# FFN2 for pairs of token tiles by seven products in a fused attention and FFN kernel

## The chip, the cores and the metric

The kernel runs on one core of a Trainium2 chip. The core has TensorE (PE: matmuls, and weight loads beside them as PEld), VectorE (DVE), ScalarE (ACT), GpSimd (POOL) and SyncE (SP, here a queue that issues DMAs). Each engine works through its own list of instructions in order and waits on semaphores for the others. The metric is the device time in microseconds (us), the median of several runs.

## The reference, cut to what matters

There are 8 batches, 12 heads, 448 positions and a head width of 64; the FFN takes the 3584 tokens of all batches, 768 wide, to 2048 and back.

```python
scores = q @ k.T / sqrt(64)
attn   = max(scores, 0) ** 2 / 448
x      = (attn @ v) with heads put side by side     # 3584 x 768
h      = x @ w_in                                   # 3584 x 2048
g      = max(h, 0) + alpha * min(h, 0)
out    = g @ w_out                                  # 3584 x 768
```

## The kernel before, in words

**Stages.** A "quad" is four heads of one batch; there are three in a batch (NG) and 24 in all. For a quad the kernel loads q, k and v as bf16 (`load_qk`, `load_v`: DMAs of GpSimd's queue), turns q and k so that the head width lies on partitions, computes seven score chunks of 128 x 896 (`score_mm`, L184), passes each through a relu on ScalarE (L193) or VectorE (L195), squares it on VectorE (L203), multiplies by v (`attnv`, L213), and writes xT with the scale, half on ScalarE (L223), half on VectorE (L224).

For a batch, `f1` then runs 16 times (index ff, one block of 128 of d_ff each): six matmuls of 448 columns (L247), `neg` = relu(-h) on ScalarE (L255), and gT = beta * neg + h on VectorE (L256). Two batches share one gT, of 128 x 16 x 896 in bf16, which holds seven token tiles of 128. `f2` takes one token tile and one of two column ranges (256 or 512 wide, `COLS`), accumulates 16 matmuls into a bank (L272), copies it with ScalarE to an `o` tile (L274) and stores it in two halves through Sync's queue (L280).

**Turning q and k.** Quads 0 to 4 are transposed on TensorE. From quad 5 on `turn_dma` first copies q and k into a `perm` tile with VectorE (L170, two copies), and then Sync issues one transposing DMA from `perm` into T (L172). `perm` has three buffers. Three one-element GpSimd copies to `landed` (L425, L473, L488) hold GpSimd's queue until the transposes of quads 5, 6 and 8 have landed; the next loads stand behind them.

**Order of the work.** The order is written out by hand (`manual_schedule`), and every engine runs its instructions in the order of the code. From batch 2 on, FFN1 of a batch is cut by two runs of three score chunks (before ff 6 and ff 12) and has two `prepare` calls (ff 1 and 9), each of which turns one quad and loads another. The FFN2 stage after it has three bursts, one for each quad of the next batch: three score chunks with relus on ScalarE, VectorE, ScalarE ("ADA"), the product with v, two more chunks ("AD"), and then the squares of the five chunks. The stage after an even batch works on token tiles 0 to 2 and the one after an odd batch on tiles 3 to 6. Batch 7 has no bursts.

**PSUM.** There are eight banks of 512 F32. `take_bank` and `take_pair` choose the bank, or the even-aligned pair, that was taken least recently; a score chunk and an attention product each need a pair, FFN1 and FFN2 a bank. `hold` sets a bank aside.

## Time and profile before

| What | Value |
|---|---|
| Median of 3 runs | 386.65 us (385.65 to 386.66) |
| Profiled execution, first to last instruction | 384.0 us |
| Granted TensorE clock | 1.000 |
| TensorE busy | 374.1 us |
| VectorE, ScalarE, GpSimd busy | 266.2, 207.6, 68.9 us |
| FFN2 stage after batch 2 (137.52 to 160.62) | 23.10 us, VectorE busy 17.71 |
| FFN2 stage after batch 3 (180.38 to 208.68) | 28.30 us, VectorE busy 17.79 |
| FFN2 stage after batch 6 (319.35 to 341.31) | 21.96 us, VectorE busy 11.03 |
| FFN2 of batch 7 (from 359.47) | about 21.1 us |

The profile shows one execution. Its own time is known as the span from the first instruction to the last; the medians are of other executions and include what lies around the span. In a line of a group the fields are line, engine, operation, output and inputs, shape and count, then the busy time in us, the mean ns of one, and the engine's idle time just before them with what ended it. In a line of the timeline they are start, duration, line, operation and count, with the idle time before in square brackets. Matmuls overlap, so that the mean of one is longer than the distance between two starts.

### The profile page before, as it was taken

The page shows a single profiled execution, that of the slowest core. Times are in us where ns is not written, and L with a number is a line of the kernel's source. Part 1 is how long each engine was busy: PE and PEld are TensorE (multiplying, and loading weights), DVE is VectorE, ACT ScalarE, POOL GpSimd, SP SyncE. Part 2 cuts the span into 40 slices and gives each one's busy share as a digit, 9 for nine tenths or more (in the row PEclk, how much of TensorE's full clock was granted, in tenths as well). Part 3 has the DMA queues.
Part 4 walks back from the last instruction along what each step waited for, and adds up shares of the span by engine and source line. Part 5 has one row for each costly group of instructions (what it writes and reads, how often), then busy time and mean ns, then how long its engine had stood idle before and what let it go on. Part 6 is the DMA issues. An engine that isn't in the chain of part 4 may idle for free.

```text
span 384.0 us, 7838 instructions
## 1 busy us (share of the span) xinstructions
PE 374.1 (97%) x3171; PEld 205.3 (53%) x3192; DVE 266.2 (69%) x423; ACT 207.6 (54%) x335; POOL 68.9 (18%) x105
## 2 busy tenths in 40 slices
PE   6799999999999999999999999999999999999996
PEld 5454565555544455545565455544556445645554
DVE  3987988777657988688656887779855788526300
ACT  4988687445643754455444656546544475434321
POOL 8566050506402202022200222020000000000000
PEclk9999999999999999999999999999999999999999
DMA  9999989999995667488292772946035300120023
GB/s 145 192 204 202 186 127 199 171 178 203 224 172 109 108 113 114 105 134 119 48 167 60 134 120 53 165 76 120 15 86 88 77 1 15 43 68 2 14 68 85
DMA packets 73556, 43.29 MB, mean 113 GB/s; under 512 B 40368, under 2 KB 70064, under 8 KB 73520
## 3 DMA queue, kind: packets, MB, share of 16 engines
q0 software_dynamic: 27136, 22.58, 39.8%
q1 hardware_dynamic: 45952, 19.88, 26.8%
q8 instruction: 25, 0.41, 0.5%
q10 hardware_dynamic: 432, 0.33, 0.3%
q14 instruction: 11, 0.09, 0.1%
HBM read 45.62 MB, written 11.01 MB: 147 GB/s over the span
## 4 chain that ended last, share of the span: by engine, by line
PE 95%; DVE 2%; issue 1%; POOL 0%; ACT 0%; ACTq 0%; POOLq 0%; DVEq 0%
PE psum L247 38%; PE psum L272 38%; PE psum L184 9%; PE psum L213 8%; DVE at L203 1%; PE psum L146 1%; DVE T L165 1%; PE psum L162 1%; DVE rl L195 0%; POOL kraw L131 0%; ACT osb L274 0%; ACTq L280 0%; POOL ident masks.py:199 0%; POOL ident masks.py:197 0%; POOLq masks.py:199 0%
## 5 line engine op out<-in xcount | busy, mean ns | idle before, releaser
L272 PE MATMUL psum<-w_out,gT 128*128 128x256 bf16 (+3 forms) x891 | 149.8, 322 | 1.1
L247 PE MATMUL psum<-xT,w_in_sb 128*128 128x448 bf16 x768 | 149.8, 353 | 0.0
L272 PEld LDWEIGHTS <-gT 128*128 128x128 bf16 x912 | 86.8, 98 | 64.2 <-issue 8.2
L247 PEld LDWEIGHTS <-w_in_sb 128*128 128x128 bf16 x768 | 73.7, 98 | 72.8 <-issue 5.3
L256 DVE SCALAR_TENSOR_TENSOR gT<-neg,beta_sb,psum 128x448 bf16<-128x448 f32 x128 | 83.4, 676 | 33.8 <-ACT neg L255 33.6
L255 ACT ACTIVATE neg<-psum 128x448 f32<-128x448 f32 x128 | 69.2, 546 | 60.3 <-PE psum L247 59.2
L193 ACT ACTIVATE rl<-psum 128x896 bf16<-128x896 f32 x112 | 97.7, 930 | 1.4 <-PE psum L184 1.4
L203 DVE TENSOR_TENSOR at<-rl 128x896 bf16<-128x896 bf16 x162 | 90.5, 616 | 0.0
L195 DVE TENSOR_SCALAR rl<-psum 128x896 bf16<-128x896 f32 x56 | 60.8, 1085 | 40.4 <-PE psum L184 40.3
L274 ACT COPY osb<-psum 128x256 f32<-128x256 f32 (+3 forms) x57 | 26.9, 473 | 104.7 <-PE psum L272 97.6
L184 PE MATMUL psum<-T 64*64 64x448 bf16 x672 | 45.4, 356 | 2.1 <-DVE T L165 1.1
L100 POOL DMA_DIRECT2D qraw<-in_q_dram x23 | 16.6, 722 | 136.2 <-DVE perm L170 131.7
L213 PE MATMUL psum<-at,vraw 64*64 64x448 bf16 x672 | 36.2, 350 | 0.0
L184 PEld LDWEIGHTS <-T 64*64 64x64 bf16 x672 | 16.8, 105 | 21.0 <-issue 13.6
L213 PEld LDWEIGHTS <-vraw 64*64 64x64 bf16 x672 | 21.0, 106 | 11.7 <-issue 1.5
L224 DVE TENSOR_SCALAR xT<-psum 128x448 bf16<-128x448 f32 x24 | 15.0, 624 | 14.8 <-PE psum L213 11.0
L107 POOL DMA_DIRECT2D vraw<-in_v_dram x24 | 17.5, 732 | 4.6 <-PE psum L184 1.4
L100 POOL DMA_DIRECT2D kraw<-in_k_dram x23 | 16.7, 726 | 1.9 <-issue 1.4
L223 ACT ACTIVATE xT<-psum 128x448 bf16<-128x448 f32 x24 | 13.4, 560 | 2.3 <-PE psum L213 2.3
L170 DVE COPY perm<-qraw 128x896 bf16<-128x896 bf16 x19 | 11.6, 610 | 0.0
L170 DVE COPY perm<-kraw 128x896 bf16<-128x896 bf16 x19 | 11.6, 608 | 0.0
L117 POOL DMA_DIRECT2D w_in_sb<-in_moe_w_in_dram x16 | 10.0, 634 | 5.5 <-DMA w_in_sb<-in_moe_w_in_dram 2.3
(24 smaller groups left out, 41.6 us busy)
## 6 DMA issues: line engine op xcount, KB each, us to landing
out_dram<-osb SPq DMA_DIRECT2D x54, 128.0 KB, 2.4
vraw<-in_v_dram POOLq DMA_DIRECT2D x24, 224.0 KB, 8.5
qraw<-in_q_dram POOLq DMA_DIRECT2D x23, 224.0 KB, 4.7
kraw<-in_k_dram POOLq DMA_DIRECT2D x23, 224.0 KB, 6.9
out_dram<-osb SPq DMA_DIRECT2D x56, 64.0 KB, 2.3
w_in_sb<-in_moe_w_in_dram POOLq DMA_DIRECT2D x16, 192.0 KB, 8.1
w_out<-in_moe_w_out_dram POOLq DMA_DIRECT2D x4, 512.0 KB, 10.3
w_out<-in_moe_w_out_dram POOLq DMA_DIRECT2D x4, 256.0 KB, 8.6
```

What stands on the lines that cost most here:

```text
L100: nc.gpsimd.dma_start(out=t.rearrange("p m j d -> p m (j d)"), in_=flat[:, 2 * g:2 * g + 2])
L170: nc.vector.tensor_copy(p[:, i], raw.pop((n, name)).rearrange("p s j d -> p j s d"))
L184: nc.tensor.matmul(ps[64 * c:64 * c + 64, r, :S], t[64 * r:64 * r + 64, 1, j, 64 * c:64 * c + 64], t[64 * r:64 * r + 64, 0, :, 64 * c:64 * ...
L193: nc.scalar.activation(rl, ps[:, :, :S], ACTF.Relu)
L195: nc.vector.tensor_scalar(rl, ps[:, :, :S], 0.0, None, ALU.max)
L203: nc.vector.tensor_tensor(a, rl, rl, ALU.mult)
L213: nc.tensor.matmul(ps[64 * s:64 * s + 64, r, :S], vv[64 * r:64 * r + 64, s, j, :], a[64 * r:64 * r + 64, s], start=(j == 0), stop=(j == NJ ...
L247: nc.tensor.matmul(ps, w_in_sb[:, km // 2, km % 2, bass.ts(ff, 128)], xT[b][:, km // 2, km % 2, :], start=(km == 0), stop=(km == KM - 1))
L255: nc.scalar.activation(neg, ps, ACTF.Relu, scale=-1.0)
L256: nc.vector.scalar_tensor_tensor(gT[b // 2][:, ff, (b % 2) * S:(b % 2) * S + S], neg, beta_sb[:, ff:ff + 1], ps, ALU.mult, ALU.add)
L272: nc.tensor.matmul(ps, gT[sb][:, ff, bass.ts(c, 128)], w_out_sb[h][:, ff, lo:hi], start=(ff == 0), stop=(ff == KF - 1))
L274: nc.scalar.copy(o[:, lo:hi], ps)
```

## The change

FFN2 of batches 2 to 7 goes through a new class `Pair` for pairs of token tiles. With a pair's gT split in four quarters (two tiles a and b, two halves of d_ff) and w_out split in four (two halves of d_ff, two halves of the 768 columns), a product of two by two blocks is made with seven block products and not eight (the Winograd form of Strassen's scheme). Each block product is eight matmuls of 384 columns. Four sums and differences of gT quarters are made on VectorE for each pair (`mix`), four of w_out once (`weight_mix`, in eight pieces, in the stage after batch 1). The results are gathered by accumulating products in three PSUM banks (x, y, z) and by adding the copy m1 or the sums u2 and u3 with VectorE (`plus`, five for each pair); ScalarE copies twice for each pair. There are three pairs for each two batches; the seventh token tile still goes through `f2`. x and y are one bank pair, held from p1 to p4; z is an ordinary `take_bank`.

Of the relus from batch 2 on only the third of each first burst stays on VectorE ("AAD", "AAA", then "AA", "AAA"); FFN1 has two runs, of three and two chunks (two and two in batch 2). The copies into `perm` go to GpSimd for quads 9 and later. `w_out_sb` is one tile. Several pools get fewer buffers; `perm` has one, not three. Two new pools come in, u (4) and S (4); S also takes some of the early `at` tiles, and the first q tiles come from the o pool.

```diff
-    perm_pool = ctx.enter_context(tc.tile_pool(name="perm", bufs=3))
+    perm_pool = ctx.enter_context(tc.tile_pool(name="perm", bufs=1))
-    rl_pool = ctx.enter_context(tc.tile_pool(name="rl", bufs=7))
-    at_pool = ctx.enter_context(tc.tile_pool(name="at", bufs=12))
+    rl_pool = ctx.enter_context(tc.tile_pool(name="rl", bufs=6))
+    at_pool = ctx.enter_context(tc.tile_pool(name="at", bufs=10))
-    neg_pool = ctx.enter_context(tc.tile_pool(name="neg", bufs=3))
-    o_pool = ctx.enter_context(tc.tile_pool(name="o", bufs=10))
+    neg_pool = ctx.enter_context(tc.tile_pool(name="neg", bufs=2))
+    o_pool = ctx.enter_context(tc.tile_pool(name="o", bufs=6))
+    u_pool = ctx.enter_context(tc.tile_pool(name="u", bufs=4))
+    S_pool = ctx.enter_context(tc.tile_pool(name="S", bufs=4))
...
+    def hold_pair():
+        lo = min((0, 2, 4, 6), key=lambda i: (max(taken[i], taken[i + 1]), i))
+        taken[lo] = taken[lo + 1] = 10**9
+        return lo
...
-            nc.vector.tensor_copy(p[:, i], raw.pop((n, name)).rearrange("p s j d -> p j s d"))
+            (nc.gpsimd if n > 2 * NG + 2 else nc.vector).tensor_copy(p[:, i], raw.pop((n, name)).rearrange("p s j d -> p j s d"))
...
+        def mix(self, *which):
+            for i in which:
+                t = self.s[i] = S_pool.tile([128, KH, 128], BF16, tag="S", name="S")
+                x, y, op = {1: (self.a21, self.a22, ALU.add),
+                            2: (self.s.get(1), self.a11, ALU.subtract),
+                            3: (self.a11, self.a21, ALU.subtract),
+                            4: (self.a12, self.s.get(2), ALU.subtract)}[i]
+                nc.vector.tensor_tensor(t, x, y, op)
+        def mm(self, ps, left, right, start):
+            for i in range(KH):
+                nc.tensor.matmul(ps, left[:, i], right[:, i], start=(start and i == 0), stop=(i == KH - 1),
+                                 skip_group_check=not start)
+        def p1(self):
+            self.xy = hold_pair()
+            self.x, self.y = psum[:, self.xy, :NH], psum[:, self.xy + 1, :NH]
+            self.mm(self.x, self.a11, w_out_sb[:, :KH, :NH], True)
+            self.m1 = self.kept()
+            nc.scalar.copy(self.m1, self.x)
+        def p6(self):
+            self.mm(self.y, self.s[2], w_mix[1], True)
+            self.u2 = self.plus(self.y, self.m1, self.kept())
+        def p7(self):
+            self.mm(self.y, self.s[3], w_mix[2], False)
+            self.u3 = self.plus(self.y, self.m1, self.kept())
+        def p5(self):
+            self.z = take_bank()[:, :NH]
+            self.mm(self.z, self.s[1], w_mix[0], True)
+        def c22(self):
+            store(self.sb, self.tb, NH, d_model, self.plus(self.z, self.u3))
+        def p2(self):
+            self.mm(self.x, self.a12, w_out_sb[:, KH:, :NH], False)
...
+        def p4(self):
+            self.mm(self.y, self.a22, w_mix[3], False)
+            take(self.xy, 2)
+            store(self.sb, self.tb, 0, NH, self.plus(self.y, self.m1))
+        def p3(self):
+            self.mm(self.z, self.s[4], w_out_sb[:, KH:, NH:], False)
+            store(self.sb, self.ta, NH, d_model, self.plus(self.z, self.u2))
+        def tail(self):
+            self.p7(); self.p5(); self.c22(); self.p2(); self.p4(); self.p3()
...
         if b % 2 == 0:
+            p = Pair(sb, 0, 1)
+            p.mix(1, 2)
+            if b + 2 < B:
+                f2(sb, 2, 0)
+            p.mix(3, 4)
+            burst(n0, "AAD", "AAA")
+            prepare(n0 + 4)
+            p.p1()
+            p.p6()
+            burst(n0 + 1, "AA", "AAA")
+            if b + 2 < B:
+                p.tail()
+                burst(n0 + 2, "AA", "AAA")
+                f2(sb, 2, 1)
...
+        elif not last:
+            p, r = Pair(sb, 3, 4), Pair(sb, 5, 6)
+            p.mix(1, 2, 3, 4)
+            burst(n0, "AAD", "AAA")
+            prepare(n0 + 4)
+            p.p1()
+            p.p6()
+            burst(n0 + 1, "AA", "AAA")
+            p.tail()
+            r.mix(1, 2, 3, 4)
+            r.p1()
+            r.p6()
+            burst(n0 + 2, "AA", "AAA")
+            r.tail()
         else:
+            p, r = Pair(sb, 2, 3), Pair(sb, 4, 5)
+            p.mix(1, 2, 3, 4)
+            p.p1(); p.p6(); p.p5(); p.p2(); p.p7(); p.c22()
+            f2(sb, 6, 0)
+            p.p4(); p.p3()
+            r.mix(1, 2, 3, 4)
+            r.p1(); r.p6(); r.p5(); r.p2(); r.p7(); r.c22(); r.p4(); r.p3()
+            f2(sb, 6, 1, parts=((0, 384), (384, 512)))
```

In the diff some calls that stand on lines of their own are put on one line.

## The prediction, made before the result was known

> **What bounds the kernel now.** I read the page's busy shares and its chain first, then the groups by shape, then the timeline of one FFN2 stage on all engines, then the Vector and Sync queues around the four transposing transfers of the first stages. The page:
>
> ```profile
> span 384.0 us, 7838 instructions
> ...
> PE 374.1 (97%) x3171; PEld 205.3 (53%) x3192; DVE 266.2 (69%) x423; ACT 207.6 (54%) x335; POOL 68.9 (18%) x105
> ...
> PE 95%; DVE 2%; issue 1%; POOL 0%; ACT 0%; ACTq 0%; POOLq 0%; DVEq 0%
> ```
>
> TensorE is busy 97% and carries 95% of the chain: a matmul saved is time saved, and a TensorE wait is time lost, since nothing gives it back. The groups by shape (busy us, mean ns):
>
> ```profile
> L272 PE MATMUL psum<-w_out,gT 128*128 128x512 bf16 x411 | 95.8, 379 | 1.1
> L203 DVE TENSOR_TENSOR at<-rl 128x896 bf16<-128x896 bf16 x162 | 90.5, 616 | 0.0
> ...
> L256 DVE SCALAR_TENSOR_TENSOR gT<-neg,beta_sb,psum 128x448 bf16<-128x448 f32 x128 | 83.4, 676 | 33.8 <-ACT neg L255 33.6
> ```
>
> A mean includes the pipeline; what counts is the spacing of starts. The timeline of the stage after FFN1 of batch 3 (start, us):
>
> ```profile
> 180.38 1.91 PE L272 MATMUL psum<-w_out,gT 128*128 128x256 bf16 x16
> 180.58 0.55 ACT L255 ACTIVATE neg<-psum 128x448 f32<-128x448 f32 x1 [0.59 <-PE psum L247]
> 181.16 0.68 DVE L256 SCALAR_TENSOR_TENSOR gT<-neg,beta_sb,psum 128x448 bf16<-128x448 f32 x1 [0.28 <-ACT neg L255]
> ...
> 182.22 0.76 PE L184 MATMUL psum<-T 64*64 64x448 bf16 x12
> ...
> 182.65 1.73 ACT L193 ACTIVATE rl<-psum 128x896 bf16<-128x896 f32 x2
> ...
> 182.81 1.50 PE L213 MATMUL psum<-at,vraw 64*64 64x448 bf16 x28
> 182.84 1.09 DVE L195 TENSOR_SCALAR rl<-psum 128x896 bf16<-128x896 f32 x1 [1.00 <-PE psum L184]
> ...
> 184.13 0.55 PE L184 MATMUL psum<-T 64*64 64x448 bf16 x8
> ```
>
> The last gT of FFN1 is ready 1.46 us after TensorE has left FFN1 (180.38 to 181.84); a score chunk costs TensorE 0.20, the attention product 1.33 (182.81 to 184.13); a relu starts 0.43 after its chunk, and two on ScalarE take 1.73. No engine is late here. Vector, Sync and GpSimd in batch 1:
>
> ```profile
> 63.71 0.61 DVE L170 COPY perm<-qraw 128x896 bf16<-128x896 bf16 x1
> ...
> 71.44 0.61 DVE L170 COPY perm<-qraw 128x896 bf16<-128x896 bf16 x1
> ```
> ```profile
> 64.91 2.46 SPq L172 DMA_TRANSPOSE T<-perm  x1
> ```
> ```profile
> 67.40 0.18 POOL L473 COPY landed<-T 1x1 bf16<-1x1 bf16 x1 [12.41 <-DMA T<-perm]
> 67.85 2.23 POOL L122 DMA_DIRECT2D w_out<-in_moe_w_out_dram  x3 [0.27 <-issue]
> ...
> 87.35 0.18 POOL L488 COPY landed<-T 1x1 bf16<-1x1 bf16 x1 [14.42 <-DMA T<-perm]
> ```
>
> Quad 6's transpose has landed at 67.4; quad 7's copy was made at 63.7, into another of three buffers.
>
> **TensorE saves 11.9.** A 256-wide pass of 16 matmuls takes 1.84 (180.38 to 182.22), a 512-wide one 3.46 (337.85 to 341.31): 5.30 a tile, 10.60 a pair. A 384-wide pass lies midway, 2.65, so a product of 8 costs 1.325, and 7 cost 9.27. Nine pairs (three for each two batches): 9 x 1.33 = -11.9. Attention and FFN1 issue the same matmuls.
>
> **Stage starts cost 10.2.** Everything below is counted from TensorE's end of FFN1. Vector must end gT (1.46), then the four operand additions, before the one relu that stays on it ("D" third in the first burst). An addition is a square (spacing 0.535) on 1024 in place of 896 elements: 0.61; the second waits for the first's result, so they run 1.5 to 4.0 and the relu to 5.1. ScalarE's relus are done earlier. The burst's sixth chunk takes the third chunk's bank pair again (four pairs, least recent first), at 3 x 0.2 + 1.33 + 2 x 0.2 = 2.33 if nothing is late. It starts at 5.15: 2.8 lost, less a little slack, 2.75. That is so after batches 3, 5 and 6 (8.25). After 2 and 4 a 256-wide pass stands first, so 0.95 each (1.9). Lower end: the addition costs a square's 0.535, -0.3 each. Upper end: it runs as slowly as the Vector relu (1085 ns for 896, so 1.2), +2.4 each. I take 0.61: same operation and types, 128 more elements.
>
> **Held banks cost 5.9.** x and y hold one bank pair through a burst, so three remain. Such a burst is two chunks, the attention product and three chunks. Of the three the second waits for the second relu (0.43 + 1.73 after the burst's start), and the third for the xT copy behind that relu (0.56, L223): it starts at 2.8 or a little later, not at 2.13, 0.65 lost. Seven such bursts (one each after 2, 4, 6; two after 3, 5): 4.6. After 2 and 4 the third burst's attention product asks for the pair with z while its last add is unread, and the next pass waits for an xT copy: 0.65 x 2 = 1.3. Ends 0 and 0.9 a burst.
>
> **Chains through Vector cost 5.0.** An add of PSUM and u over 384 F32 is the gT row cut from 448: 0.6. A second pair's p6 needs: PSUM out 0.2, last add 0.6, additions 0.6 and 0.7, against one product of cover (1.325): 0.85 lost, after 3 and 5 (1.7). In batch 7 there are no bursts: the first p6 waits to 2.9 where it was due at 1.3 (1.6), the second pair's p6 0.85, and its p4 stands right behind p7, whose add it needs, 0.85: 3.3. Ends 0.6 and 1.5 of the size.
>
> **One perm buffer costs 4.4.** In batch 1 the copies of quad 7 (Vector, at 63.7) now wait for quad 6's landing at 67.4. Behind them stand gT(2) and all later ones. Eight banks let TensorE run to ff 10, which then waits 0.95. Quad 7's transpose issues at 68.5, not 64.9, in the midst of the w_out and q, k, v loads begun at 67.85. Quad 8's copies, again on Vector and due at about 74.3, wait for its landing, and behind them gT(11) to gT(15), which the next FFN2 pass needs. The landing: 4.0 us without loads (quad 7 before), 6.2 to 7.6 beside three small loads, 11.6 after three loads and stores, 14.6 amid the same seven loads (quad 8 before). I take 9, the middle of these rows, as only the first of the seven loads is ahead of it: 77.5, copies to 78.6, five gTs at 0.62 to 81.75, the pass ends at 82.0, not 77.6: +4.4. Ends: +0.95 (landed by 74.3) and +9.9 (14.6). The Trainium skill (DMA: Bandwidth & Descriptors, Queues, rings and completion order) has each DMA engine go round between its queues a packet at a time; a transpose of many small packets would then wait beside the loads to their end, as the 14.6 row did, and the sum would be 407 by the rule, 402 by my middle.
>
> **The small terms.** Eight weight additions of 1536 elements on Vector (0.87 each by the square's slope), in the stage after batch 1: the one ahead of the burst of quad 6 makes its relu late by 0.65; the others lie in passes of 1.84 to 3.46 with Vector idle. Without that cover each costs up to 0.87. The 30 perm copies on GpSimd: no row shows one. The two nearest are 178 ns for 1 element (L473) and 287 for 128 (the identity's select), a slope of 0.85 ns, so 0.94 each. Their queue holds only loads, each issued two quads ahead; Sync's transpose waits for them where it waited for Vector, with stores behind it only 8 us later. So they are free, unless they slow Vector: none to two copies at each of five stage starts, 0 to 9.4; I take 1.0, as they most often end before the additions begin. Here a rule speaks against the change. The Trainium skill (SBUF — State Buffer, Who interferes with whom) says that a Vector instruction with two SBUF inputs and a GpSimd one that reads SBUF lock each other out for a whole instruction. By it the sum would be up to 410, by the rows of this trace, which show no such meeting, 401 to 402; no run here shows it yet. Fewer relus and no perm copies on Vector help FFN1 stages, where TensorE waits for nothing now: 0. ScalarE has 32 relus more (37 on Vector in batches 2 to 6 become 5) and takes them in its idle time (10 of 20 us). The smaller pools (at 10, o 6, rl 6, neg 2) cover what is alive at once; 0, or up to 1 where a store is late.
>
> **Sum.** -11.9 + 10.2 + 5.9 + 5.0 + 4.4 + 0.65 + 1.0 = +15.2. The profiled span of 384.0 goes to 399.2; the median of the runs stands 2.65 above the span, so 386.65 goes to 401.8.
>
> **Rivals.**
> Transposes amid loads take their longest: the 14.6 row is the same traffic; against it, quad 7's starts earlier in it. +5.5: 407.
> GpSimd locks Vector out at each stage start: 0.94 x 2 x 5 in place of 1.0: 410. Nothing measured speaks for it or against.
> Quad 7's transpose lands in time and the bursts lose nothing (the page shows no ScalarE wait in the bursts now): -3.45 - 4.6: 394.
> Faster: Vector does not run in the written order but takes what is ready, so a relu or gT is never behind an addition or a waiting copy. Then 10.2, 1.7 of the chains and 4.4 go, 10.8 of waits stay, and 385.5 at most, 383 if the bursts lose half. It decides once the waits sum to under 11.9. Against it: in the trace Vector's relus and squares stand in the order of the code.
> The change does not do what it says: matmuls not fewer; excluded by the count, 56 for 64.
>
> **How the numbers follow.** My forecast (398 to 406) 0.50; long transposes 0.15; locks 0.10; the mild case (390 to 397) 0.12; Vector not in order or waits overcounted, 0.13, of which 0.10 under 385.5 and 0.03 within. A measurement tells 0.3% (1.2 us) from no change: faster 0.10, same 0.03, slower 0.87. The range 389.5 to 411 leaves out the faster and equal cases.
>
> **What would show it.** Right: TensorE's idle time rises by about 25 us, in gaps of 1 to 3 us at the stage starts, ended by the Vector relu and gT; the 384-wide pass shows 0.166 us a matmul; Vector waits for a transpose's landing twice between 63 and 82. Wrong: additions well under 0.6, a sixth chunk that does not wait, or quad 7's landing before 74.

## The result, and the profile after

The changed kernel takes 411.63 us (median of 4 runs, 410.45 to 412.40) where the kernel before takes 386.61 (385.65 to 386.66): 1.0654 times as long, 95% interval 1.0633 to 1.0676. The profiled execution has a span of 409.84 us against 384.04, 25.8 more. The direction was forecast, and the size was not: 401.8 was said, with 411.0 as the upper end.

The page of the changed kernel, busy shares, clock row and chain by engine:

```profile
span 409.8 us, 7791 instructions
PE 375.2 (92%) x3120; PEld 200.7 (49%) x3120; DVE 283.4 (69%) x450; ACT 225.1 (55%) x349; POOL 98.3 (24%) x135
PEclk9999999958999999999999999999999999999999
PE 75%; DVE 12%; DMA 5%; ACT 4%; issue 2%; POOL 0%; ACTq 0%; DVEq 0%; POOLq 0%
```

TensorE's time outside its busy time went from 9.9 us (384.0 - 374.1) to 34.6 (409.8 - 375.2): 24.7 more idle time. VectorE's share of the chain rose from 2% to 12%, and transfers, which were not on it, have 5%. One slice of the clock row shows 5 and one 8: for a while TensorE ran at half clock.

Where the time came from is read from the spacing of FFN1. In this table, worked out from the traces, a stage runs from the start of a batch's last FFN1 matmul to the start of the next batch's first (for batch 7 to the end of the span), in us. The experiments are in it as well, since most of their reading is here. A score chunk takes TensorE 0.20, and the kernels divide the chunks between stages and FFN1 differently: before has 15 in each of b2 to b5, after has 16, and e6, e7, e10 and e14 have 13 in b3 and b5, with more of them in the FFN1 of batches 4 and 6, which is 0.8 to 1.0 us longer than after's. So small differences between these rows are partly a matter of where the chunks stand.

| Kernel | b1 | b2 | b3 | b4 | b5 | b6 | b7 |
|---|---|---|---|---|---|---|---|
| before | 42.21 | 23.29 | 28.49 | 23.29 | 28.49 | 22.16 | 24.75 |
| after | 56.49 | 24.26 | 30.93 | 24.26 | 32.61 | 19.41 | 31.03 |
| e1 quad 7's own buffer | 45.42 | 24.26 | 30.93 | 24.31 | 30.93 | 21.08 | 31.02 |
| e2 loads later | 51.01 | 24.26 | 31.45 | 24.26 | 33.13 | 19.40 | 31.03 |
| e3 first relu to ScalarE | 46.47 | 24.06 | 29.47 | 24.16 | 29.93 | 17.57 | 31.05 |
| e4 no additions | 46.78 | 23.33 | 28.50 | 23.71 | 28.65 | 17.44 | 28.53 |
| e5 copies on VectorE | 42.82 | 24.37 | 31.04 | 24.91 | 31.04 | 19.41 | 30.73 |
| e6 reordered | 42.82 | 25.66 | 27.84 | 25.66 | 27.40 | 18.07 | 27.35 |
| e7 reordered, VectorE | 42.82 | 25.25 | 27.50 | 25.25 | 27.50 | 18.07 | 27.34 |
| e8 copies alone | 44.73 | 23.29 | 28.49 | 23.29 | 28.49 | 22.16 | 25.41 |
| e9 three undone | 42.83 | 24.06 | 28.24 | 24.16 | 28.24 | 17.57 | 28.22 |
| e10 reordered again | 42.82 | 24.41 | 28.06 | 24.41 | 28.25 | 23.42 | 23.08 |
| e11 relus alone | 42.21 | 25.12 | 30.32 | 25.12 | 30.32 | 22.77 | 24.72 |
| e12 three undone, alternating | 42.82 | 26.97 | 30.16 | 26.28 | 30.16 | 18.50 | 28.23 |
| e13 relus undone | 42.82 | 26.41 | 34.70 | 29.08 | 34.70 | 20.51 | 30.74 |
| e14 blocks | 42.82 | 23.11 | 26.67 | 23.11 | 26.67 | 22.48 | 23.11 |

After against before: b1 +14.28, b2 and b4 +0.97 each, b3 +2.44, b5 +4.12, b6 and b7 together +3.53 (a tile of FFN2 moved from b6 to b7, so only their sum can be compared). That is 26.3; FFN1 itself moved by less than 1 us a batch. More than half of the loss lies in the one stage of batch 1.

**Batch 1.** VectorE's timeline of the changed kernel:

```profile
67.78 0.62 DVE L179 COPY perm<-qraw 128x896 bf16<-128x896 bf16 x1 [4.23 <-DMA T<-perm]
...
68.85 6.08 DVE L268 SCALAR_TENSOR_TENSOR gT<-neg,beta_sb,psum 128x448 bf16<-128x448 f32 x9
84.84 0.62 DVE L179 COPY perm<-qraw 128x896 bf16<-128x896 bf16 x1 [9.92 <-DMA T<-perm]
```

and TensorE's:

```profile
76.38 1.36 PE L292 MATMUL psum<-w_out_sb,gT 128*128 128x256 bf16 x11
86.64 0.39 PE L292 MATMUL psum<-w_out_sb,gT 128*128 128x256 bf16 x1 [8.89 <-DVE gT L268]
```

Quad 7's copies wait 4.23 us for quad 6's transpose, and quad 8's wait 9.92 for quad 7's, which was issued at 68.99, landed at 84.72, 15.7 us later, and is waited for until 84.84. Behind quad 8's copies stand the last gTs of batch 1, and TensorE waits 8.89 for them. From 80.67 to 94.33 its granted clock was 0.5. For the first 3 us behind the gap TensorE still follows the late gTs; then the next chunks and 256-wide pass of 16 take 4.76 (89.66 to 94.42, the pass alone 3.49), not the 2.55 of before (77.58 to 80.13).

**A steady stage.** TensorE and VectorE behind FFN1 of batch 3:

```profile
195.78 0.76 PE L193 MATMUL psum<-T 64*64 64x448 bf16 x12
...
197.20 1.51 PE L225 MATMUL psum<-at,vraw 64*64 64x448 bf16 x26 [0.47 <-DVE gT L268]
198.37 0.72 PE L193 MATMUL psum<-T 64*64 64x448 bf16 x8
200.86 0.38 PE L193 MATMUL psum<-T 64*64 64x448 bf16 x4 [1.77 <-DVE rl L204]
```
```profile
197.18 0.69 DVE L322 TENSOR_TENSOR S<-gT 128x1024 bf16<-128x1024 bf16 x1
197.91 0.69 DVE L322 TENSOR_TENSOR S<-S,gT 128x1024 bf16<-128x1024 bf16 x1
198.52 0.68 DVE L322 TENSOR_TENSOR S<-gT 128x1024 bf16<-128x1024 bf16 x1
199.12 0.68 DVE L322 TENSOR_TENSOR S<-gT,S 128x1024 bf16<-128x1024 bf16 x1
199.72 1.08 DVE L204 TENSOR_SCALAR rl<-psum 128x896 bf16<-128x896 f32 x1
```

TensorE left FFN1 at 195.78. The additions follow the last gT 1.4 us later, the relu stands behind all four, and the sixth chunk waits for it until 200.86, 5.1 after the start. The second pair's sixth product (p6) of this stage waits 0.68 us for its additions, at 215.49.

### The profile page after: what moved, and what is told of

The parts are those of the page before. It is cut to its first block, busy times and chain, and to the rows that moved or that the text cites. A ratio compares the mean times of both kernels' runs of the same rounds, so it can differ in the third digit from the quotient of the medians.

```text
span 409.8 us, 7791 instructions
## 1 busy us (share of the span) xinstructions
PE 375.2 (92%) x3120; PEld 200.7 (49%) x3120; DVE 283.4 (69%) x450; ACT 225.1 (55%) x349; POOL 98.3 (24%) x135
## 4 chain that ended last, share of the span: by engine, by line
PE 75%; DVE 12%; DMA 5%; ACT 4%; issue 2%; POOL 0%; ACTq 0%; DVEq 0%; POOLq 0%
PE psum L259 33%; PE psum L326 20%; PE psum L292 12%; PE psum L193 6%; DMA T<-perm 5%; DVE S L322 4%; PE psum L225 4%; DVE rl L204 2%; DVE gT L268 2%; ACT rl L202 1%; DVE at L215 1%; ACT xT L235 1%; ACT neg L267 1%; PE psum L155 1%; DVE osb L331 1%
## 5 line engine op out<-in xcount | busy, mean ns | idle before, releaser
L202 ACT ACTIVATE rl<-psum 128x896 bf16<-128x896 f32 x144 | 124.2, 934 | 19.0 <-PE psum L193 19.0
L292 PE MATMUL psum<-w_out_sb,gT 128*128 128x256 bf16 (+3 forms) x336 | 57.8, 327 | 10.1 <-DVE gT L268 10.0
L292 PEld LDWEIGHTS <-gT 128*128 128x128 bf16 x336 | 32.5, 100 | 35.0 <-DVE gT L268 11.5
L179 POOL COPY perm<-qraw 128x896 bf16<-128x896 bf16 x15 | 15.0, 1001 | 132.2 <-DMA T<-perm 132.2
L326 PE MATMUL psum<-w_mix,S 128*128 128x384 bf16 x216 | 39.3, 332 | 3.5 <-DVE S L322 3.5
L326 PEld LDWEIGHTS <-S 128*128 128x128 bf16 x288 | 27.6, 99 | 24.8 <-DVE S L322 5.1
L204 DVE TENSOR_SCALAR rl<-psum 128x896 bf16<-128x896 f32 x24 | 26.1, 1086 | 10.0 <-PE psum L193 8.7
L294 ACT COPY osb<-psum 128x256 f32<-128x256 f32 (+3 forms) x21 | 9.7, 462 | 40.4 <-PE psum L292 37.8
L331 DVE TENSOR_TENSOR osb<-psum,u 128x384 f32<-128x384 f32 x27 | 15.1, 557 | 20.1 <-PE psum L326 18.7
L326 PEld LDWEIGHTS <-gT 128*128 128x128 bf16 x216 | 20.9, 98 | 15.4 <-issue 2.2
L326 PE MATMUL psum<-w_out_sb,gT 128*128 128x384 bf16 x144 | 27.1, 333 | 0.0
L116 POOL DMA_DIRECT2D vraw<-in_v_dram x24 | 17.5, 730 | 13.6 <-PE psum L193 11.9
```

The lines of the kernel that those rows point to most:

```text
L116: nc.gpsimd.dma_start(out=t.rearrange("p m j d -> p m (j d)"), in_=flat[:, 2 * g:2 * g + 2])
L202: nc.scalar.activation(rl, ps[:, :, :S], ACTF.Relu)
L204: nc.vector.tensor_scalar(rl, ps[:, :, :S], 0.0, None, ALU.max)
L292: nc.tensor.matmul(ps, gT[sb][:, ff, bass.ts(c, 128)], w_out_sb[:, ff, first_col + lo:first_col + hi], start=(ff == 0), stop=(ff == KF - 1))
L326: nc.tensor.matmul(ps, left[:, i], right[:, i], start=(start and i == 0), stop=(i == KH - 1), skip_group_check=not start)
L331: nc.vector.tensor_tensor(t, ps, u, ALU.add)
```

## The experiments

Each ratio below is to the kernel before on the same chip. The first four start from the changed kernel.

### Quad 7 gets a perm buffer of its own (e1)

```diff
     def turn_dma(n):
-        p = perm_pool.tile([128, 2, NJ, 2, D], BF16, tag="perm", name="perm")
+        if n == 7:
+            p = w_mix[3].rearrange("p k c -> p (k c)")[:, :4 * NJ * D].rearrange(...)
+        else:
+            p = perm_pool.tile([128, 2, NJ, 2, D], BF16, tag="perm", name="perm")
```

The fourth weight tile is idle until the stage behind.

> The changed kernel with one thing different: quad 7's copy goes into w_mix[3], which is idle until the end of the stage after batch 1, so that the one perm buffer makes no VectorE copy wait there. Buffer theory: the FFN2 pass after batch 1 no longer ends 13 us late (89.66 against about 77), nor is the clock halved after it; of the 411.6 us some 14.3 go: 397.3 (396 to 399). Rival, the loads and not the buffer hold things up (the transposes would land late whatever holds the copy): no more than 2 us go, 409 to 412.

Measured: 401.37 us (399.45 to 404.50), ratio 1.0408 (1.0355 to 1.0460), 10.3 less than the changed kernel. VectorE's copies of quads 7 and 8 wait for nothing any more, the half clock there is gone, and b1 falls from 56.49 to 45.42. The time is 4.1 above the 397.3 expected, and b1 is still 3.2 above before. Most of that is at quad 9, GpSimd's first (another 0.42 is a relu behind a weight addition), by the timelines of GpSimd and of TensorE:

```profile
88.28 0.18 POOL L591 COPY landed<-T 1x1 bf16<-1x1 bf16 x1 [14.26 <-DMA T<-perm]
...
91.96 0.73 POOL L116 DMA_DIRECT2D vraw<-in_v_dram  x1 [0.35 <-PE psum L196]
92.68 1.03 POOL L182 COPY perm<-qraw 128x896 bf16<-128x896 bf16 x1
93.66 0.93 POOL L182 COPY perm<-kraw 128x896 bf16<-128x896 bf16 x1
```
```profile
108.53 0.38 PE L196 MATMUL psum<-T 64*64 64x448 bf16 x4 [2.40 <-DMA T<-perm]
```

The copies now stand in GpSimd's queue behind the copy to `landed`, which waits for quad 8's transpose until 88.3, and behind the issue of five loads; on VectorE they were made at 83.4. The transpose is issued at 94.6 (86.4 before), and the first chunk of quad 9 waits 2.40 us for it. This profile also has a half-clock stretch of 3.4 us in b6, worth 1.7, which the changed kernel's has in b5.

### One buffer kept, the loads behind quad 7's transpose (e2)

```diff
-            nc.gpsimd.tensor_copy(landed, T[6][:1, 0, 0, :1])
-            load_w_out(1, 4)
-            ...
         if ff in (1, 10):
             turn_dma(7 + ff // 9)
+        if ff == 1:
+            nc.gpsimd.tensor_copy(landed, T[7][:1, 0, 0, :1])
+            load_w_out(1, 4)
+            ...
```

> One perm buffer kept; the loads that GpSimd starts when quad 6's transpose has landed start when quad 7's has landed. Theory of the landing amid loads: quad 7's transpose lands in 4 to 6 us, not 15.7, so quad 8's copy does not wait; the first wait of 4 us on VectorE stays and costs TensorE under 1 us; w_out's second columns land some 5 us later, which may cost FFN2 up to 3 us: 399 (397 to 402). Rival, one buffer costs this much whatever the loads do: 409 to 412.

Measured: 406.57 us (404.19 to 407.38), ratio 1.0524 (1.0488 to 1.0560). GpSimd's and Sync's queues:

```profile
72.92 0.18 POOL L583 COPY landed<-T 1x1 bf16<-1x1 bf16 x1 [17.44 <-DMA T<-perm]
```
```profile
68.74 1.52 SPq L181 DMA_TRANSPOSE T<-perm  x1
```

Without the loads the same transpose, issued at 68.74, has landed by 72.9, some 4.2 us, and the wait of 9.92 is gone: what was long was the landing amid the loads. The run takes all seven loads away together. Which of them are in the way is seen in the changed kernel's trace: two were issued ahead of the transpose (68.24 and 68.97) and five behind it, and of those five the ones issued at 69.70 and 70.43 landed before it (82.45 and 83.99, the transpose at 84.72). The time expected (399) was missed by 7.6 us, because the loads that were put off meet quad 8's transpose (16.0 us to landing), and so make quad 9 late in its turn: its transpose is issued at 98.16 and TensorE waits 4.51 us for it at 111.74, with 6.8 us of half clock around that wait.

### The relu behind the additions to ScalarE (e3)

e1, and in even and odd batches

```diff
-            burst(n0, "AAD", "AAA")
+            burst(n0, "AAA", "AAA")
```

> On top of e1: the third relu of each first burst on ScalarE too, so that no relu stands behind the four operand additions on VectorE. Theory of the relu behind the additions: after batches 3, 5 and 6 the sixth chunk starts at about 3.4 us after FFN1, not 5.1, 1.75 less each; after 2 and 4 ScalarE's third relu ends no earlier than VectorE's did, 0: e1 less 5.2, 392 (and 1.7 less again if the half clock after batch 5 does not come back). Rival, ScalarE's longer row of relus makes the later copies late by as much: as e1, 396 to 398.

Measured: 395.35 us (392.13 to 395.71), ratio 1.0220 (1.0171 to 1.0268): 6.0 less than e1. b3 and b5 are shorter by 1.46 and 1.0, b6 by 3.5 (1.7 of it the half clock of e1's profile), b2 and b4 by 0.2; b1 is 1.05 longer, with a wait of 2.42 and a half-clock stretch behind it. In b3 and b5 the gain is smaller than the wait of 1.77 taken away, since the relu now stands third in ScalarE's row.

### The additions of gT's halves left out (e4)

e1, and the products read gT itself:

```diff
-                t = self.s[i] = S_pool.tile([128, KH, 128], BF16, tag="S", name="S")
-                ...
-                nc.vector.tensor_tensor(t, x, y, op)
+                self.s[i] = {1: self.a21, 2: self.a11, 3: self.a21, 4: self.a12}[i]
```

> On top of e1: the four operand additions of each pair are left out; plain quarters of gT stand in their place, so FFN2 of the pairs computes something else (that part of the work is missing). Theory that VectorE's chains set the waits: 1.9 less after 3, 5 and 6, 0.7 less after 2 and 4, 0.85 less for each second pair after 3 and 5, 2.2 less in batch 7: e1 less 11, 386 (384 to 388). Rival, the waits come from the held banks and the order of TensorE's own list: e1 less 3 at most, 394 or more.

Measured: 389.26 us (388.34 to 389.96), ratio 1.0084 (1.0061 to 1.0108). The additions and what stands behind them cost 12.1 us, where 11 was expected. By stage b2 to b7 give back 12.4, of which 1.7 is the half clock of e1's b6, and b1 is 1.4 longer, with a late relu (2.69). What is left still is not faster than before.

### All copies back on VectorE (e5)

e1, quad 9 into the third weight tile as well, and

```diff
-            (nc.gpsimd if n > 2 * NG + 2 else nc.vector).tensor_copy(...)
+            nc.vector.tensor_copy(...)
```

> The kernel with quad 7's own perm buffer, with all copies ahead of transposing transfers back on VectorE and quad 9's perm buffer in a further idle tile. Theory (copies on GpSimd cost batch 1 its lock and its late transposes, and buy nothing in the steady stages, where the half of VectorE that they free is not what is late): batch 1's stage goes from 45.4 back to 42.3 to 42.8, its squares stay at 0.56 us each, batches 2 to 5 lie within 0.5 us of 24.3 and 30.9; together 396.5 to 399.5. Rival (the copies' 1.07 us of a quad are work that VectorE can't take on in the new order): batches 3, 5 and 6 grow by 1 us or more each, 401 or above. Rival (the chain of batch 1 is late for another reason): batch 1 stays at 45.

Measured: 399.44 us (397.64 to 400.58), ratio 1.0345 (1.0309 to 1.0381). b1 is at 42.82, 2.6 under e1; b2 to b5 differ from e1 by 0.1 to 0.6. Close to the theory: GpSimd's copies cost batch 1, and buy at most 0.6 a stage elsewhere. Two things change here, the engine of the copies and quad 9's buffer; the next run changes the engine alone, in the kernel before.

### GpSimd's copies alone, in the kernel before (e8)

```diff
-            nc.vector.tensor_copy(p[:, i], raw.pop((n, name)).rearrange("p s j d -> p j s d"))
+            (nc.gpsimd if n > 2 * NG + 2 else nc.vector).tensor_copy(p[:, i], ...)
```

> The kernel before with one part of the change alone: copies ahead of transposing transfers on GpSimd from quad 9 on, three perm buffers kept, everything else as before. Theory (a lock of squares and late transposes in batch 1, nothing in the steady stages): batch 1's stage grows by 2 to 4 us, the others by under 0.3 each, together 388.5 to 391.5. Rival (GpSimd's copies are hidden): 385 to 387. Rival (freeing VectorE makes the steady stages shorter): below 385.

Measured: 388.91 us (388.40 to 389.13), ratio 1.0075 (1.0060 to 1.0090). b1 grows by 2.52, b2 to b6 by nothing at all; the 0.66 more of b7 lie behind TensorE's last matmul. GpSimd's, VectorE's and TensorE's timelines in b1:

```profile
90.70 0.95 POOL L170 COPY perm<-qraw 128x896 bf16<-128x896 bf16 x1
91.57 0.94 POOL L170 COPY perm<-kraw 128x896 bf16<-128x896 bf16 x1
```
```profile
89.48 3.52 DVE L203 TENSOR_TENSOR at<-rl 128x896 bf16<-128x896 bf16 x3
92.93 1.08 DVE L195 TENSOR_SCALAR rl<-psum 128x896 bf16<-128x896 f32 x1
```
```profile
94.06 0.38 PE L184 MATMUL psum<-T 64*64 64x448 bf16 x4 [1.39 <-DVE rl L195]
```

In the kernel before, the same three squares took 1.69 us. With the two copies' 1.89 that makes 3.58, and 3.52 is what they take now: the two engines took turns. The relu behind them is late, and TensorE waits 1.39 for it; another 0.74 it waits for quad 9's transpose, at 106.94. Over the whole kernel the 162 squares are busy for 98.5 us, 8.0 more than before, and in the steady stages none of it is seen, because TensorE doesn't wait for VectorE there. The Trainium skill (SBUF — State Buffer, Who interferes with whom) states such an exclusive lock for a VectorE instruction with two SBUF inputs and a GpSimd one that reads SBUF; these rows agree with it.

### The same arithmetic in another order (e6, e7)

e5 with products of a pair between the halves of a burst, the additions of a second pair ahead of the products of the first, some relus back on VectorE, and other counts of chunks in FFN1. The core of it, for the even batches:

```diff
-            p = Pair(sb, 0, 1)
-            ...
-            p.mix(3, 4)
-            burst(n0, "AAD", "AAA")
+            p.mix(1, 2)
+            p.p1()
+            sc(some(2, "AA"))
+            attnv(n0)
+            p.mix(3)
+            p.p6()
+            p.mix(4)
+            sc(some(3, "AAA"))
+            sq()
+            p.p2()
+            p.p7()
```

e6 has the copies from quad 11 on on GpSimd, e7 all on VectorE.

> All of the change's arithmetic (seven products for the pairs of batches 2 to 7), with its own perm buffers for quads 7 and 9 and copies on GpSimd from quad 11 on, but the steady batches written out in another order: the products whose operand needs one VectorE addition stand between the halves of a burst, a second pair's additions are issued ahead of the products of the first, no burst holds a bank for a relu behind additions, and f1 meets chunks of scores at its blocks 3, 8 and 12. Theory (the seven products save 11.9 us on TensorE, and what eats them is where the chains of additions stand): b2 and b4 at 22 to 23, b3 and b5 at 26 to 27.5, the last stage at 26 to 28, together 374 to 382, faster than before by 1 to 3%. Rival (the additions make VectorE late wherever they stand, or the extra weight loads of narrow passes eat the gain): 384 to 392.

> The reordered kernel with all copies ahead of transposes on VectorE. Theory (GpSimd's copies buy nothing): within 1 us of the reordered kernel. Rival (with the additions there, VectorE has no room for 1.07 us more of each quad): 3 us or more above it. Rival (GpSimd's copies and VectorE's two-input operations stretch one another): 1 to 3 us below it.

Measured: e6 387.81 us (387.08 to 389.62), ratio 1.0047 (1.0030 to 1.0065); e7 388.23 (387.83 to 388.43), ratio 1.0057 (1.0042 to 1.0072). The odd stages and batch 7 gain 3 to 4 us each against e5 (0.6 of it in an odd stage is three chunks moved to the next FFN1), b6 gains 1.3, b2 and b4 lose 0.3 to 1.3. Both are 23 to 24 us faster than the changed kernel, but the gain expected over before did not come, and both lie in the range of e6's first rival. Where the copies are made doesn't matter, as the theory had it.

### All suspected costs taken away at once (e9)

e5, with the edits of e3 and e4.

> The changed kernel with every suspected cost taken away at once: own perm buffers for quads 7 and 9 and all copies on VectorE, the first bursts' relus all on ScalarE, and the additions of gT's halves left out (part of the computation is missing: the products read gT itself). What stays of the change is the seven products, the additions of the weights and those behind the products. Theory (the costs add up: 11.9 us saved, and the perm buffer, the copies, the relu behind additions and the chains of additions are all that eats it): 378 to 383. Rival (something else of the change costs too, such as weight loads of narrower passes or VectorE's additions after the products): 386 or above.

Measured: 385.91 us (384.96 to 387.23), ratio 0.9984 (0.9971 to 0.9997). The theory that these costs explain everything falls: of the 11.9 us that the products save, 0.7 comes back. The time lies just below the rival's 386. TensorE in the first two bursts of batch 2:

```profile
140.31 0.76 PE L196 MATMUL psum<-T 64*64 64x448 bf16 x12
...
143.33 0.38 PE L196 MATMUL psum<-T 64*64 64x448 bf16 x4 [0.43 <-ACT rl L205]
143.77 1.46 PE L324 MATMUL psum<-w_out_sb,gT 128*128 128x384 bf16 x8
...
146.46 0.57 PE L196 MATMUL psum<-T 64*64 64x448 bf16 x8
146.86 1.49 PE L228 MATMUL psum<-at,vraw 64*64 64x448 bf16 x28
148.19 1.30 PE L196 MATMUL psum<-T 64*64 64x448 bf16 x12
149.42 2.77 PE L324 MATMUL psum<-w_mix,gT 128*128 128x384 bf16 x16
```

A burst lasts from its first chunk to the next pass or product. The three of the stage take 3.46 (140.31 to 143.77), 2.96 (146.46 to 149.42) and 2.86, where each took 2.40 before; the first has a sixth chunk now, 0.20 of its time. That is 2.1 us a stage, all that b2 is missing: it should be at 23.29 - 1.33, and is at 24.06. b3 is 2.4 above 28.49 - 2.65. No addition of gT stands before the bursts here. In the first burst, the longest, no bank pair is held yet, and its last chunk waits for a relu on ScalarE.

### A second order, made from that profile (e10)

e7 with every half of a burst between products, batch 6 like batches 2 and 4, batch 7 as two pairs, and the copies of the stage moved to its end.

> The complete arithmetic of the change again, all copies on VectorE, in an order made from the profile of the reordered kernel: in batches 2 to 6 every half of a burst has a product of 1.3 us or a pass between it and the next, the product behind p7 no longer waits for an addition that stands behind five squares (0.81 us each time there), batch 6 takes tile 2 as batches 2 and 4 do, and batch 7 is two pairs whose first products stand together ahead of their additions. Theory (the gain is there when the chains are covered): b2, b4 and b6 at 22.0 to 22.8, b3 and b5 at 26 to 26.8, b7 at 21.8 to 22.6, together 374 to 380, faster than before by 2 to 3%. Rival (VectorE has no room: 21 to 23 us of work in stages of 22): b2 and b4 at 24 or above, together 383 to 388.

Measured: 397.08 us (395.69 to 397.62), ratio 1.0267 (1.0245 to 1.0290). The time lies above theory and rival alike. 7.6 us of it lie inside FFN1 of batch 3 (26.95 long, 19.38 in e7): moved to the stage's end, the copies come 12 us later than in e7, and the next quad's copies wait for their transpose's landing. VectorE there:

```profile
172.35 0.62 DVE L182 COPY perm<-qraw 128x896 bf16<-128x896 bf16 x1 [7.05 <-DMA T<-perm]
```

It is the perm buffer's wait of batch 1 once more, with a gap of 4.14 on TensorE and 6.8 us of half clock around it. b2 and b4 stay at 24.41, where the rival has them.

### Relus on ScalarE alone, in the kernel before (e11)

```diff
-        return [... in zip(chunks[lo:at_c[0]], "ADA")]
+        return [... in zip(chunks[lo:at_c[0]], "AAA" if lo >= 27 else "ADA")]
```

> The kernel before with one part of the change alone: from batch 2 on all relus of scores on ScalarE. Theory (five relus of 0.85 us in a row on ScalarE are longer than the 2.4 us that TensorE needs for a burst, so it waits for banks): each burst of batches 2 to 6 grows by 0.4 to 0.7 us, 15 bursts, together 392 to 397. Rival (the passes around the bursts give ScalarE the time, and VectorE is relieved): 384 to 388.

Measured: 394.25 us (393.75 to 394.52), ratio 1.0214 (1.0198 to 1.0229). TensorE in batch 2:

```profile
148.47 0.76 PE L184 MATMUL psum<-T 64*64 64x448 bf16 x12
149.06 1.49 PE L213 MATMUL psum<-at,vraw 64*64 64x448 bf16 x28
150.38 0.68 PE L184 MATMUL psum<-T 64*64 64x448 bf16 x8
151.49 5.36 PE L272 MATMUL psum<-w_out,gT 128*128 128x512 bf16 x32 [0.43 <-ACT rl L193]
```

Here no bank is held, there is no addition and no pair, and a burst takes 3.02 us (148.47 to 151.49) where it took 2.40. Five relus of 0.85 and an xT copy in a row on ScalarE are longer than the burst, and the next pass waits for a bank. This part alone costs 8.3 us. In e9 the burst with a held pair took 2.96; without one it takes 3.02, so the held banks explain nothing that ScalarE's row doesn't; no run frees the held pair alone. In b6 and b7 of e9 together 2.9 us stay (45.79 for 46.91 - 4.0) that no run took apart; 0.4 of it is two more chunks in b6.

### Relus alternating again (e12, e13)

e12 is e9, and e13 is e5, with the relus of batches 2 to 6 as in the kernel before:

```diff
-            burst(n0, "AAA", "AAA")
+            burst(n0, "ADA", "ADA")
-            burst(n0 + 1, "AA", "AAA")
+            burst(n0 + 1, "AD", "ADA")
```

(e13 has "AAD" in the first line removed. The third bursts and the chunks in FFN1 change in the same way.)

> The kernel with the three suspected costs undone (own perm buffers, copies on VectorE, additions of gT's halves left out, so that part of the computation is missing), and now the relus of batches 2 to 6 alternating between ScalarE and VectorE as in the kernel before. Theory (relus on ScalarE alone eat the rest): bursts back to 2.4 to 2.6 us each, b2 and b4 at 22 to 22.8, b3 and b5 at 26 to 27, together 376 to 381. Rival (the banks held over the bursts do it): within 1.5 us of 385.9.

> The changed kernel, complete in its arithmetic, with own perm buffers, copies on VectorE, and the relus of batches 2 to 6 alternating as in the kernel before. Theory (VectorE then has relus, squares and additions in one queue, and every relu behind additions holds a bank for 1 to 3 us): slower than the 399.4 us with relus on ScalarE, 401 to 408. Rival (alternating is better with the additions too): 390 to 397.

Measured: e12 395.86 us (395.54 to 397.61), ratio 1.0272 (1.0245 to 1.0299); e13 409.75 (408.37 to 411.42), ratio 1.0619 (1.0587 to 1.0651). e12's theory falls, and its rival too: alternating is 10 us slower than ScalarE alone in this order of work, while it is 8.3 us faster in the order before. VectorE and TensorE in e12's batch 2 show why:

```profile
146.64 0.61 DVE L182 COPY perm<-qraw 128x896 bf16<-128x896 bf16 x1
...
147.70 0.54 DVE L329 TENSOR_TENSOR u<-psum,u 128x384 f32<-128x384 f32 x1
148.16 1.08 DVE L207 TENSOR_SCALAR rl<-psum 128x896 bf16<-128x896 f32 x1
```
```profile
149.29 1.11 PE L196 MATMUL psum<-T 64*64 64x448 bf16 x8 [2.07 <-DVE rl L207]
```

The relu of a chunk that was ready at about 145.5 starts at 148.16, behind six squares, two copies and an addition, because only two products (2.7 us) lie between this burst and the one before, where there were passes of 5.3 us. TensorE waits 2.07 us for it, and a half-clock stretch of 3.41 follows. So relus mostly on ScalarE were the lesser evil of this order. e13 went as its theory had it, a little beyond its upper end, with three half-clock stretches of 3.41 in its profile.

### Pairs in one block, passes between the bursts (e14)

The complete arithmetic again. In even batches tile 2 is cut into three passes of 256 columns, which stand ahead of, between and behind the bursts; the seven products of the pair stand together with no burst inside; relus alternate where VectorE is free; copies behind FFN1 are on ScalarE. In odd batches products stand between the halves of the bursts, batch 6 goes as batches 2 and 4, and batch 7 is two pairs, as in e10.

```diff
+                f2(sb, 2, 0, parts=HALVES[:1])
+                sc(some(3, "AAD"))
+                attnv(n0)
+                sc(some(2, "AD"))
+                ...
+                p.p1()
+                p.p6()
+                ...
+                p.p3()
+                burst(n0 + 1, "AAD", "AA")
+                f2(sb, 2, 0, parts=HALVES[1:2])
+                ...
+                f2(sb, 2, 0, parts=HALVES[2:])
```

> The complete arithmetic in a third order: in even batches the seven products of a pair stand together with no burst inside, and tile 2 is cut into three passes of 256 columns that stand ahead of, between and behind the bursts, so that no bank is held over a burst and the additions are covered by a pass; in the steady stages copies on ScalarE, where it idles behind the products; batch 6 as batches 2 and 4, batch 7 two pairs. Theory (what eats the gain is waits of bursts, and a pass between them removes it): b2, b4 at 22 to 22.8, b3, b5 at 26 to 27, b6 and b7 together 43.5 to 45.5, in all 377 to 382, faster than before by 1 to 2.5%. Rival (the gain can't be had beside VectorE's additions in any order): 385 or above.

Measured: 382.72 us (381.96 to 383.15), ratio 0.9914 (0.9897 to 0.9932): faster than both kernels, by 0.9% against before and by 29 us against the changed one. Its page and batch 2 on TensorE:

```profile
span 380.4 us, 7912 instructions
PE 368.3 (97%) x3160; PEld 203.2 (53%) x3160; DVE 296.1 (78%) x481; ACT 224.6 (59%) x351; POOL 68.9 (18%) x105
```
```profile
139.65 0.76 PE L196 MATMUL psum<-T 64*64 64x448 bf16 x12
...
142.18 1.47 PE L327 MATMUL psum<-w_out_sb,gT 128*128 128x384 bf16 x8
...
151.38 1.10 PE L196 MATMUL psum<-T 64*64 64x448 bf16 x12
...
154.12 1.92 PE L294 MATMUL psum<-w_out_sb,gT 128*128 128x256 bf16 x16
155.97 0.76 PE L196 MATMUL psum<-T 64*64 64x448 bf16 x12
...
158.99 1.91 PE L294 MATMUL psum<-w_out_sb,gT 128*128 128x256 bf16 x16 [0.20 <-ACT rl L205]
```

The first burst takes 2.53 (139.65 to 142.18), with four additions of gT in the same stage; the other two still take 2.74 (151.38 to 154.12) and 3.02 (155.97 to 158.99), and tile 2 in three passes takes 5.52 for 5.30. So of the 1.33 that the pair saves in this stage little comes back, and of the 11.9 in all, 3.2. The time is a little above what was expected (377 to 382): b2 and b4 are at 23.11, not at 22 to 22.8. The run changes order, passes, relus and copies at once, and which of them brought the gain is not shown.

## Why the prediction was right or wrong

**The step that failed: "I take 9".** The term "One perm buffer costs 4.4" had the right mechanism in both its waits, and it sized the second wrongly. The landing of quad 7's transpose was taken from the middle of rows between 4.0 and 14.6 us, with the reason that only the first of the seven loads is ahead of it. It took 15.7, longer than the longest row; without the loads the same transfer took some 4.2 (e2). So the reason didn't hold: being issued ahead of most of the loads didn't let it land ahead of them, as loads issued after it landed first. By the upper end (+9.9) the sum would have been 407, which was a rival at 0.15 and is the mechanism that held. The first chunk behind the pass is 12.1 late (89.66 for 77.58), 2.2 more than that end, mostly because the landing came later than the longest row; half clock makes it 14.3 by the next pass (94.42 for 80.13) and it is still 14.3 at 102.12. The half clock is in no term of the prediction. With 14.3 in place of 4.4 the prediction's own sum is a span of 409.1, against 409.84 measured; that the median then comes to 411.7, with 411.63 measured, is luck in the last step, as the runs of the changed kernel stand 1.9 to 2.0 above their spans and not 2.65. Taking the cause away gives back 10.3 in all and 11.1 in b1, not 14.3 (e1), since quad 9's lateness, hidden behind the gap, then comes to light.

**TensorE saves 11.9: right.** A block of seven products takes 9.20 in e14 (142.18 to the next chunk at 151.38), predicted 9.27. So the narrower passes with their weight loads cost no more than was said, and that part of the rivals of e6 and e9 falls.

**Stage starts cost 10.2: right as a time, partly wrong as a cause.** The relu was to end at 5.1 after FFN1 and the sixth chunk to start then; measured 5.0 and 5.1, additions 0.69 each with starts 0.6 to 0.7 apart. But of the 2.75 put on this after b3, moving the relu gives back only 1.46 (e3): in its place three relus in a row keep ScalarE late.

**Held banks cost 5.9: right size a burst, wrong cause.** The forecast was 0.65 for such a burst, measured 0.56 (e9). The held pair has no part in it that shows: e11 has all pairs free and loses 0.62 a burst. It is ScalarE's row of five relus, and so bursts without a held pair lose it too (0.86 in e9's first, beside its sixth chunk). This is the prediction's other failed step: it had ScalarE take its 32 more relus "in its idle time" at no cost, and in the kernel before they cost 8.3 alone. That the 5.9 of another term stood in for it is luck.

**Chains through Vector cost 5.0: about right.** With the stage starts it made 15.2; e4 takes all additions away and gains 12.1, of which about 10.7 by stage once half clock is left aside. The difference may be time that ScalarE's relus take when the additions are gone; no run shows it. The second pair's first wait was put at 0.85, though its parts (0.2, 0.6, 0.6 and 0.7, less 1.325) add up to 0.78, and it measured 0.68. Batch 7 was put at 3.3; its three waits come to 2.84 (1.51, 0.68 and 0.65), and it lost 2.5 by e4.

**GpSimd locks 1.0: in the wrong place.** "None to two copies at each of five stage starts" cost nothing there (e8: b2 to b5 unchanged). In the kernel before, the copies cost 2.5 us in batch 1, by the lock (1.39) and by a late transpose of quad 9 (0.74); with the rest of the change, putting them back, with quad 9's own buffer, gains 1.9 (e5 against e1). The prediction saw Sync waiting "for them where it waited for Vector" and missed that GpSimd's own queue puts the wait for quad 8 and the issue of loads ahead of them. The copy itself was well estimated: 0.94, measured 0.93 to 0.95 undisturbed.

**By stage** the terms add up to +0.92 for b2 and b4 (measured 0.97), +2.25 for b3 and b5 (2.44; 4.12 with a half-clock stretch of 3.4 us in b5), +2.7 for b6 and b7 together (3.53). In b1 the terms make 5.05 and 14.28 was measured, so 9.2 of the 10.6 us that the span was off are one landing and the clock behind it. The weight additions were put at 0.65 there, and e5, with the waits of b1 gone, has b1 0.61 above before. The sign "TensorE's idle time rises by about 25 us" came true at 24.7, but not as it was meant: it was to be gaps of 1 to 3 us, and one gap alone has 8.89.

**The rivals.** Long transposes held. The lock is real, but costs nothing at the stage starts, where the rival priced it. The mild case and VectorE out of order fall: its rows stand in the order of the code.

## What to carry to other kernels

A cut in matmuls is worth its time only where the order still covers what the cut adds: the same seven products gave +25 us with the order and buffers of the change and -3.2 with those of e14, of 11.9 saved on TensorE. Which engine takes a relu can't be chosen by itself: ScalarE alone cost 8.3 us in one order and saved 10 in another, and in e12 the difference was how many microseconds of pass lie between two bursts of work for VectorE. A buffer taken from a transfer that runs amid loads is priced at that transfer's longest landing, not at a middle, plus the clock that a long gap costs.

## What the runs showed of the hardware beyond expectation

- The granted clock fell to 0.5 around gaps of TensorE, in stretches of whole multiples of 3.41 us (the last stretch of each run, behind its last matmuls, is left aside): 13.65 us around the gap of 8.89 (after), 6.83 around gaps of 4.51 (e2) and 4.14 (e10), 3.41 after gaps of 2.42 (e3) and 2.69 (e4). Gaps of 1.8 to 2.4 brought it on in some cases and not in others: 1.77 at 293 us of the changed kernel did, 1.77 at 199 us of it did not, and neither did 2.40 in e1. The Trainium skill (TensorE: Matmul & The Clock Gate, Part 1: The HAM clock gate) speaks of a free-running window of about 3.4 us; the multiples agree with that. It puts the loss of clock after at least one idle window of about 3.4 us; here gaps shorter than that were enough.
- A transposing transfer of one quad landed in about 4.2 us alone (e2, quad 7) and in 13.5 to 15.7 amid loads (quad 7 in the changed kernel, quad 9 in e1 and e2); for quad 7 five of the seven loads were issued after it, and two of these landed before it.
- GpSimd copies and VectorE operations with two SBUF inputs excluded each other for whole instructions (e8: 3.52 us for work of 1.69 and 1.89), and 8.0 us of it in all cost the kernel only where TensorE was waiting for VectorE.
